# Moving every tile behind a constant by 64 bytes, so that the activations' tiles begin at multiples of 512 bytes

## The chip, the cores and the metric

The kernel runs on one core of one Trainium2 chip. The metric is the device time of one execution in microseconds (us), lower is better. All sizes are float32 unless said otherwise.

## What is computed

A light convolution (a causal filter of 7 taps along the sequence, one filter per head, its weights a softmax over the taps) is followed by a feed-forward layer with a smooth gate. The shapes are x: 8 x 4096 x 192, weight: 8 x 7, w_in: 192 x 2048, w_out: 2048 x 192; so there are 32768 tokens of 192 channels.

```python
def _attn_ref(x, weight):                       # B=8, S=4096, D=192, H=8, K=7
    w = softmax(weight, axis=-1)
    x_pad = np.concatenate([zeros((B, K - 1, D)), x], axis=1)
    idx = np.arange(S)[:, None] + np.arange(K)[None, :]
    x_unf = x_pad[:, idx, :].reshape(B, S, K, H, D // H)
    return np.einsum('hk,bskhg->bshg', w, x_unf).reshape(B, S, D)

def _moe_ref(x, w_in, w_out):
    h = x @ w_in
    g = np.where(h >= 1, h, np.where(h <= -1, 0.0, (h + 1) ** 2 / 4))
    return g @ w_out
```

## The kernel before

**Tiling.** The 32768 tokens are cut into 64 blocks of 512 (`TB`), two blocks making one unit of the convolution; the 2048 features of the hidden layer are cut into 8 pairs of 128 (`NPAIR`). The main loop runs over 512 steps, numbered q = 0 to 511, and two more that drain it: a step is one block and one pair of features. Each step issues three things: the first product `mm1(q)` (L407: hidden features of this pair into a PSUM tile `h`), the second product `mm2` of the step two before (L447: into the PSUM accumulators `accm` and `accr`), and the gate of the present step, which ScalarE and VectorE make out of `h` by way of the SBUF tile `g` (L458 clip, L464 square, L469 max, L476 and L482 split of `g`).

**Precision.** Apart from the first block (and the first eight second products), which use plain float32, a product is made of float32r matmuls with each number split into a high and a low part: activations `hi`/`lo` (and `rhi`, `rlo`, `rh`, `rl` for the last 64 channels) in the first product, `gh`/`gl` in the second, weights in `w` and `wr`. So `mm1` has 18 matmuls in a step and `mm2` 20. Each is 64 rows of the contraction deep (`64*128` in the profile: 64 rows, 128 columns of the array), its stationary operand is 64x128 of `w`, `wr`, and its moving operand is 64x512 of an activation tile. Two matmuls that follow one another use the two halves of the partitions (`HALVES`), and so run side by side on the two halves of the array.

**Beside that.** While the products of one unit run, the convolution of the next one is computed in slots of the same steps: SyncE loads `raw` (L147 turns it into `xT` with VectorE transposes), ScalarE multiplies by a tap (L219), GpSimd adds (L230), the result is split (`hi`, `lo`) and copied to the other half of the partitions by DMAs on SyncE's queue (`hi<-hi`, `lo<-lo`). Accumulators are copied out by ScalarE (L493, L494), added by GpSimd (L496), transposed by VectorE (L519) and stored by SyncE.

**What sets the order.** The order of every engine's work is written out by hand; nothing is planned by costs. Tiles come from pools, which take their places in SBUF one behind the other in the order in which the pools are opened: `const`, `stage`, `xin`, `xw`, `xo`, `act`, `ob`. A tile of the `const` pool is therefore followed by all other pools, and its size moves them. The constant that the change touches is `whose` (L566), which says which channel belongs to which head and is read by four matmuls at the start. It is allocated with 280 columns, of which the first 256 are used:

```python
    wk = const.tile([P, 2, K], F32, name="wk")
    warm = const.tile([P, 1], F32, name="warm")
    whose = const.tile([P, 2 * P + 3 * K + 3], F32, name="whose")[:, 0:2 * P]
    ...
    ident = const.tile([P, P], F32, name="ident")
```

The places that this gives in the program before, in bytes within a partition (each tile's length is a multiple of 32 bytes in its pool):

| tiles | first place | place modulo 512 |
|---|---|---|
| `w0` to `w9`, `wr2` to `wr9`, `wf2` to `wf9` (weights) | 16512 | 128, all of them |
| `whose` | 78048 | 224 |
| `ident` | 79168 | 320 |
| `words`, `m`, `r`, `wa` (weights on their way in) | 79680 | 320 |
| `raw`, three buffers of 2176 bytes | 113472 | 320, 448, 64 |
| `xT`, two buffers of 2176 bytes | 120000 | 192, 320 |
| `y`, `p` (convolution) | 124352 | 448 |
| `hi`, `lo`, `rhi`, `rlo`, `rh`, `rl` (moving operands of the first product) | 134592 | 448, all of them |
| `gh`, `gl`, `g` (moving operands of the second product) | 175552 | 448, all of them |
| `sum`, `osb`, `t` (results on their way out) | 212416 | 448, all of them |

Parts of a weight tile begin at multiples of 512 bytes within it, so every stationary operand of the float32r matmuls begins at 128 modulo 512, and every moving operand at 448 modulo 512, 2048 bytes long.

Of the kernel before, what the change touches and what calls it, by code (L numbers as in the profile page):

```python
# [8 lines left out]
F32 = mybir.dt.float32  # L9
# [9 lines left out]
P = 128  # L19
# [11 lines left out]
def lightconv_then_ffn(ctx: ExitStack, tc: tile.TileContext, x, weight, w_in, w_out, out):  # L31
# [26 lines left out]
    H, K = weight.shape  # L58
# [13 lines left out]
    const = ctx.enter_context(tc.tile_pool(name="const", bufs=1))  # L72
# [491 lines left out]

    wk = const.tile([P, 2, K], F32, name="wk")
    warm = const.tile([P, 1], F32, name="warm")  # L566
    whose = const.tile([P, 2 * P + 3 * K + 3], F32, name="whose")[:, 0:2 * P]
    one = ob.tile([P, TB], F32, name="sum")[:, 0:P]
    small, busy = (ob.tile([P, TB // SQ, SQ], F32, name="osb").rearrange("p j b -> p (j b)")
                    for _ in range(2))  # L570
# [337 lines left out]
```

## Time and profile before

| | |
|---|---|
| three runs, us | 2256.26, 2256.51, 2256.53 (median 2256.51) |
| the profiled execution, first to last instruction, us | 2256.3 |
| PE (matmuls) busy | 2250.8 us, 100% |
| PEld (weight loads, beside the matmuls) busy | 2232.0 us, 99% |
| VectorE busy | 2103.4 us, 93% |
| ScalarE busy | 1697.6 us, 75% |
| GpSimd busy | 1168.5 us, 52% |
| 16 DMA engines busy, main queue | 25.8% |

The page gives the profiled execution its span alone. It is 0.2 us below the median of the runs, so a sum made against the span holds for the time too. A group of the profile reads: line, engine, operation, out<-in by the program's names, shapes, count | busy us in all, mean ns of one | idle time of the engine just before. The profile writes `f32` for float32r where a matmul's operand is meant; which matmuls are float32r follows from the names (`hi`, `lo`, `gh`, `gl` and the like with `w` or `wr`). The busy time of a group of matmuls is the union of its instructions, and matmuls overlap, so counts, not busy times, are added up.

### The profile page before, as it was taken

What the parts mean: (1) busy time and instruction counts of PE and PEld (TensorE: products, weight loads), DVE (VectorE), ACT (ScalarE), POOL (GpSimd) and SP (SyncE); (2) the same over time, 40 slices, a digit from 0 to 9 for tenths busy, and PEclk for the clock granted to TensorE, in tenths of its full rate; (3) what the DMA queues carried; (4) which work ended last, traced back from release to release, by engine and by line L of the source; (5) the groups of instructions that cost most, each with busy time, mean ns of one, the idle gap of its engine ahead of it and who ended that gap; (6) DMA issues with size and microseconds to landing.
All of it is one profiled execution on the core that took longest, in us unless ns stands there. A gap on an engine that the chain in (4) does not pass through costs nothing.

```text
span 2256.3 us, 48204 instructions
## 1 busy us (share of the span) xinstructions
PE 2250.8 (100%) x19646; PEld 2232.0 (99%) x19646; DVE 2103.4 (93%) x1883; ACT 1697.6 (75%) x2153; POOL 1168.5 (52%) x868
## 2 busy tenths in 40 slices
PE   9999999999999999999999999999999999999999
PEld 6999999999999999999999999999999999999999
DVE  8899999999999999999999999999999999999997
ACT  7677877778777787777877777877778777787775
POOL 1546644556445565454654455644556545565441
PEclk9999999999999999999999999999999999999999
DMA  7222222222222212222222222222222222212211
GB/s 158 49 51 46 43 44 49 51 52 39 52 48 46 53 35 51 49 49 51 39 47 47 49 51 49 40 48 45 50 53 39 51 49 46 54 34 51 49 34 24
DMA packets 442125, 110.84 MB, mean 49 GB/s; under 512 B 410288, under 2 KB 417840, under 8 KB 441904
## 3 DMA queue, kind: packets, MB, share of 16 engines
q1 hardware_dynamic: 441744, 107.66, 25.8%
q8 instruction: 155, 2.54, 0.5%
q14 instruction: 66, 0.54, 0.1%
q10 hardware_dynamic: 160, 0.10, 0.0%
HBM read 32.84 MB, written 25.17 MB: 26 GB/s over the span
## 4 chain that ended last, share of the span: by engine, by line
PE 100%; DMA 0%; DVE 0%; ACT 0%; issue 0%; DVEq 0%
PE h L407 47%; PE accm L447 30%; PE accr L447 20%; PE accr L425 1%; PE accm L425 1%; PE accr L190 0%; PE accr L407 0%; PE accm L175 0%; DMA osb<-in_weight_dram 0%; PE h L155 0%; PE accm L181 0%; PE accr L641 0%; PE h L548 0%; PE accm L407 0%; PE accr L548 0%
## 5 line engine op out<-in xcount | busy, mean ns | idle before, releaser
L230 POOL TENSOR_TENSOR y<-y,p 128x512 f32<-128x512 f32 x546 | 765.5, 1402 | 729.4 <-DVE g L469 558.6
L482 DVE TENSOR_TENSOR gl<-g,gh 128x1024 fp32r<-128x1024 f32 (+1 forms) x497 | 732.4, 1474 | 27.5 <-ACT gh L476 23.7
L407 PE MATMUL h<-hi,w 64*128 64x512 f32 x4032 | 740.6, 389 | 0.0
L464 ACT ACTIVATE g<-g 128x1024 f32<-128x1024 f32 (+1 forms) x505 | 535.2, 1060 | 241.8 <-DVE g L458 232.4
L476 ACT CAST gh<-g 128x1024 fp32r<-128x1024 f32 (+1 forms) x497 | 521.7, 1050 | 237.2 <-DVE g L469 223.6
L458 DVE TENSOR_SCALAR g<-h 128x1024 f32<-128x1024 f32 (+1 forms) x505 | 609.7, 1208 | 96.5 <-PE h L407 88.4
L469 DVE TENSOR_TENSOR g<-h,g 128x1024 f32<-128x1024 f32 (+1 forms) x505 | 613.6, 1215 | 11.9 <-ACT g L464 4.5
L447 PE MATMUL accm<-gh,w 64*128 64x512 f32 x3968 | 614.4, 388 | 0.0
L407 PEld LDWEIGHTS h<-hi,w 64*128 64x128 f32 x4032 | 580.3, 184 | 0.0
L407 PE MATMUL h<-lo,w 64*128 64x512 f32 x2016 | 555.9, 388 | 0.0
L447 PEld LDWEIGHTS accm<-gh,w 64*128 64x128 f32 x3968 | 513.1, 184 | 0.0
L447 PE MATMUL accr<-gh,wr 64*128 64x512 f32 x1984 | 387.3, 388 | 0.0
L447 PE MATMUL accm<-gl,w 64*128 64x512 f32 x1984 | 387.3, 388 | 0.0
L447 PE MATMUL accr<-gl,wr 64*128 64x512 f32 x1984 | 387.3, 388 | 0.0
L219 ACT ACTIVATE p<-xT,wk 128x512 f32<-128x512 f32 x562 | 375.0, 709 | 0.0
L407 PEld LDWEIGHTS h<-lo,w 64*128 64x128 f32 x2016 | 350.4, 184 | 0.4 <-DMA lo<-lo 0.2
L407 PE MATMUL h<-rhi,w 64*128 64x512 f32 x992 | 306.0, 388 | 0.0
L407 PE MATMUL h<-rh,w 64*128 64x512 f32 x992 | 306.0, 388 | 0.0
L447 PEld LDWEIGHTS accm<-gl,w 64*128 64x128 f32 x1984 | 286.1, 184 | 0.0
L447 PEld LDWEIGHTS accr<-gh,wr 64*128 64x128 f32 x1984 | 286.0, 184 | 0.0
L447 PEld LDWEIGHTS accr<-gl,wr 64*128 64x128 f32 x1984 | 286.0, 184 | 0.0
L496 POOL TENSOR_TENSOR sum<-t 128x512 f32<-128x512 f32 (+1 forms) x124 | 160.7, 1317 | 127.0 <-ACT t L494 127.0
(143 smaller groups left out, 1975.3 us busy)
## 6 DMA issues: line engine op xcount, KB each, us to landing
out_dram<-osb SPq DMA_DIRECT2D x366, 64.0 KB, 2.0
raw<-in_x_dram SPq DMA_DIRECT2D x334, 68.0 KB, 2.4
hi<-hi SPq DMA_DIRECT2D x126, 128.0 KB, 2.3
lo<-lo SPq DMA_DIRECT2D x126, 128.0 KB, 2.4
rhi<-rh SPq DMA_DIRECT2D x62, 128.0 KB, 2.2
rlo<-rl SPq DMA_DIRECT2D x62, 128.0 KB, 2.3
words<-in_moe_w_in_dram SPq DMA_DIRECT2D x16, 192.0 KB, 3.9
words<-in_moe_w_out_dram SPq DMA_DIRECT2D x8, 384.0 KB, 4.6
```

The costliest lines, as they stand in the source:

```text
L219: nc.scalar.mul(p, self.xT[:, SH + k:SH + k + TB], wk[:, self.wsel, k:k + 1])
L230: nc.gpsimd.tensor_add(y, y, self.product(k))
L407: nc.tensor.matmul(h[e], w[HALVES[e], c0:c0 + P], x[e][e], start=(n == 0), stop=(n == len(mms) - 1))
L425: nc.tensor.matmul(accs[s][a, i][:, c0:c0 + D], g[half, e, b * P:(b + 1) * P], w[half, e, :], start=(j == 0 and e == 0 and b % 2 == 0), st ...
L447: nc.tensor.matmul(accs[s][a, i], st, g[HALVES[i], e, :], start=(j == 0 and n == first[a]), stop=(j == NPAIR - 1 and n == last[a]))
L458: nc.vector.tensor_scalar(out=g[:, e, :], in0=hs[q][:, e, :], scalar1=-1.0, scalar2=1.0, op0=ALU.max, op1=ALU.min)
L464: nc.scalar.activation(g[:, e, :], g[:, e, :], AF.Square, bias=0.5, scale=0.5)
L469: nc.vector.tensor_tensor(out=g[:, e, :], in0=h[:, e, :], in1=g[:, e, :], op=ALU.max)
L476: nc.scalar.copy(gh[:, e, :], gs[q][:, e, :])
L482: eng.tensor_sub(gl[:, e, :], g[:, e, :], gh[:, e, :])
L496: nc.gpsimd.tensor_add(y[:, n], t[0][:, n], t[1][:, n])
```

## The change

`whose` gets 16 more columns, 64 bytes a partition, that nothing reads or writes. Nothing before it moves (the weights stay at 128 modulo 512); `ident` and everything behind it lies 64 bytes further on.

```diff
@@ -564,7 +564,7 @@
     wk = const.tile([P, 2, K], F32, name="wk")
     warm = const.tile([P, 1], F32, name="warm")
-    whose = const.tile([P, 2 * P + 3 * K + 3], F32, name="whose")[:, 0:2 * P]
+    whose = const.tile([P, 2 * P + 3 * K + 19], F32, name="whose")[:, 0:2 * P]
     one = ob.tile([P, TB], F32, name="sum")[:, 0:P]
```

| tiles | modulo 512 before | modulo 512 after |
|---|---|---|
| weights, `whose` | 128, 224 | 128, 224 |
| `ident`, `words`, `m`, `r`, `wa` | 320 | 384 |
| `raw` | 320, 448, 64 | 384, 0, 128 |
| `xT` | 192, 320 | 256, 384 |
| `y`, `p`, `hi` ... `rl`, `gh`, `gl`, `g`, `sum`, `osb`, `t` | 448 | 0 |

No instruction is added, removed or moved on any engine, and no wait changes: the lists of TensorE, VectorE, ScalarE, GpSimd and SyncE are the same in both programs but for the addresses in them.

## The prediction

> **What bounds the kernel now.** I read the page's busy times first, then the chain of work that ended last, then who waited for whom.
>
> ```profile
> span 2256.3 us, 48204 instructions
> PE 2250.8 (100%) x19646; PEld 2232.0 (99%) x19646; DVE 2103.4 (93%) x1883; ACT 1697.6 (75%) x2153; POOL 1168.5 (52%) x868
> PEclk9999999999999999999999999999999999999999
> PE 100%; DMA 0%; DVE 0%; ACT 0%; issue 0%; DVEq 0%
> ```
>
> Of 2256.3 us TensorE has matmuls in the array for 2250.8, at a granted clock of nine tenths or more in every slice, and the chain that ended last is TensorE alone. A busy PE need not be fast, so the next question is whether it ever waits. The waits of PE and PEld, with the largest of the other engines for comparison (engine, tile, line <- releaser: us in all, times, longest):
>
> ```profile
> PE accm L597 <- POOL osb L601: 1.2, 1, 1.2
> PEld h L407 <- issue: 7.1, 32, 0.2
> PEld h L407 <- DMA lo<-lo: 0.2, 1, 0.2
> DVE g L458 <- PE h L407: 88.4, 165, 1.4
> POOL y L230 <- DVE g L469: 558.6, 30, 19.0
> ```
>
> TensorE's longest wait is 1.2 us, once, before the first matmul; its weight loads have one of 0.2 us for a DMA, and 32 pieces of at most 0.2 us, 7.1 us together, that end with nothing the profile shows. It is the others that wait for TensorE (VectorE 88.4 us). So only one thing can move the time by much: the pace at which matmuls follow one another. An engine or a transfer that becomes faster changes nothing, and one that becomes slower matters only once it makes TensorE wait.
>
> The pace, from the timeline of the matmuls (start us, us, ..., count), two steps in the middle:
>
> ```profile
> 999.86 1.24 PE L447 MATMUL accm<-gh,w 64*128 64x512 f32 x8
> ...
> 1004.22 1.24 PE L447 MATMUL accm<-gh,w 64*128 64x512 f32 x8
> ...
> 1008.56 0.78 PE L447 MATMUL accm<-gh,w 64*128 64x512 f32 x4
> ```
>
> Two steps of 38 matmuls take 1008.56 - 999.86 = 8.70 us, 114.5 ns for each; as two run side by side on the two halves of the partitions, a pair of 512 columns takes 228.9 ns. And how many there are, by the groups with their shapes kept apart:
>
> ```profile
> L407 PE MATMUL h<-hi,w 64*128 64x512 f32 x4032 | 740.6, 389 | 0.0
> L407 PE MATMUL h<-lo,w 64*128 64x512 f32 x2016 | 555.9, 388 | 0.0
> L407 PE MATMUL h<-rhi,w 64*128 64x512 f32 x992 | 306.0, 388 | 0.0
> L407 PE MATMUL h<-rh,w 64*128 64x512 f32 x992 | 306.0, 388 | 0.0
> L407 PE MATMUL h<-rl,w 64*128 64x512 f32 x496 | 192.5, 388 | 0.0
> L407 PE MATMUL h<-rlo,w 64*128 64x512 f32 x496 | 192.5, 388 | 0.0
> L447 PE MATMUL accm<-gh,w 64*128 64x512 f32 x3968 | 614.4, 388 | 0.0
> L447 PE MATMUL accr<-gh,wr 64*128 64x512 f32 x1984 | 387.3, 388 | 0.0
> L447 PE MATMUL accm<-gl,w 64*128 64x512 f32 x1984 | 387.3, 388 | 0.0
> L447 PE MATMUL accr<-gl,wr 64*128 64x512 f32 x1984 | 387.3, 388 | 0.0
> ```
>
> The first six make 9024, the last four 9920, together 18944 or 9472 pairs; at 228.9 ns they are 2168 us, 96% of the span. Every one of them reads a moving operand that begins at 448 modulo 512 and a stationary operand at 128, and all ten groups have the same mean of 388 or 389 ns. So the trace of before holds no float32r matmul at another address: their price after the change has to be bounded, not read.
>
> **The change part by part.** Nothing is issued, removed or reordered, so the sum has only address terms.
>
> *Moving operands, 448 to 0 modulo 512 (18944 matmuls).* The nearest rows are the plain float32 matmuls of the first block. Their moving operands lie at two kinds of address: `hi` and `rh` at 448, and `xT` at 436 and 444 (buffer at 320, plus 116 or 124 bytes for taps 3 and 5), which isn't even a multiple of 8. First a window of the groups from 10.99 to 12.1 us, which holds those taps, then the first block's groups and timeline:
>
> ```profile
> L190 PE MATMUL accr<-xT,t 128*128 128x512 f32 x3 | 1.4, 591 | 0.0
> ```
>
> ```profile
> L407 PE MATMUL h<-rh,gh 64*128 64x512 f32 x12 | 3.1, 589 | 0.0
> ```
>
> ```profile
> 16.67 1.88 PE L407 MATMUL h<-hi,gh 64*128 64x512 f32 x8
> 18.39 1.02 PE L407 MATMUL h<-rh,gh 64*128 64x512 f32 x4
> 19.25 1.88 PE L407 MATMUL h<-hi,gh 64*128 64x512 f32 x8
> ```
>
> 591 against 589 ns: no price on the address there. But these matmuls are slower: 12 of them in 19.25 - 16.67 = 2.58 us, 430 ns a pair, so they take a column in about twice the time, and a price that is small against that could be hidden. What float32r would cost at best is half of 430, 215 ns; it takes 228.9. The excess is 13.9 ns a pair, and I can name no wait for it. The bounds for this term follow from it: down to -13.9 ns a pair if the excess is the address's doing and goes, up to +13.9 if the new address brings as much again (the only size of such a stall that the trace has). 9472 x 13.9 ns = 132 us each way. I take 0: the only rows that differ in address, 591 and 589, differ by nothing that could be told apart, and the 13.9 ns has at least one explanation that leaves addresses out. The weight loads run all the time beside the matmuls (PEld 99%), and something of them may cost a matmul that goes at full pace and be hidden behind one at half pace.
>
> *Stationary operands.* They stay at 128 modulo 512: 0 us by themselves. What changes is their distance from the moving operand, which is the second rival's matter.
>
> *VectorE, ScalarE, GpSimd.* They read and write tiles that move by 64 bytes. VectorE's three operations of a step and its transposes:
>
> ```profile
> L482 DVE TENSOR_TENSOR gl<-g,gh 128x1024 fp32r<-128x1024 f32 x495 | 731.1, 1477 | 27.1 <-ACT gh L476 23.2
> L469 DVE TENSOR_TENSOR g<-h,g 128x1024 f32<-128x1024 f32 x503 | 612.3, 1217 | 11.9 <-ACT g L464 4.5
> L458 DVE TENSOR_SCALAR g<-h 128x1024 f32<-128x1024 f32 x503 | 608.4, 1210 | 95.8 <-PE h L407 87.7
> L147 DVE STREAM_TRANSPOSE xT<-raw x95: 464/734/739, 23.8 to 2178.0; 128x544 f32<-128x544 f32 x94, 128x288 f32<-128x288 f32 x1
> ```
>
> The transposes (minimum/median/maximum ns) read `raw` from three buffers at 320, 448 and 64 and write `xT` at 192 and 320; the longest is 739 and the median 734, though the places differ by 128 bytes or more from one to the next. So VectorE shows no price on such a step, and I take 0 for all three engines. The cover if that is wrong: VectorE is idle for 2256.3 - 2103.4 = 152.9 us, so all its work could become 7% slower before TensorE must wait for it throughout; the span would then begin to follow VectorE.
>
> *DMAs.* Their SBUF side now begins at multiples of 128 bytes in `raw` and `osb` and at multiples of 512 in `hi`, `lo`.
>
> ```profile
> DMA packets 442125, 110.84 MB, mean 49 GB/s; under 512 B 410288, under 2 KB 417840, under 8 KB 441904
> q1 hardware_dynamic: 441744, 107.66, 25.8%
> raw<-in_x_dram SPq DMA_DIRECT2D x334, 68.0 KB, 2.4
> lo<-lo SPq DMA_DIRECT2D x126, 128.0 KB, 2.4
> ```
>
> The queue uses 25.8% of the engines, a load or a swap lands 2.4 us after its issue, and TensorE waited 0.2 us for one in the whole run. A gain is hidden behind the matmuls; a loss would have to outlast a step or more before it shows. 0 us, with 0.2 us as the most that can be won.
>
> *Sum.* 0 + 0 + 0 + 0: the span stays at 2256.3 us, and the time at the runs' 2256.5. To tell a change from none the measurement needs about 0.2%, 4.5 us, which here is 4.5 us / 9472 = 0.48 ns a pair. That is a fine scale: any address effect in TensorE that occurs in every matmul would be seen.
>
> **The rivals.** *Faster: the moving operand starts in the middle of what TensorE reads at once.* The excess of 13.9 ns is about a sixteenth of 215 (13.4). If a row of 2048 bytes is read in pieces of 128 bytes, an aligned one has 16, and one that starts at 448 = 3 x 128 + 64 touches 17. Seventeen sixteenths of 215 is 228.4, beside the measured 228.9. After the change every moving operand begins at a multiple of 128 and would have 16. At half pace the extra piece would be hidden, which fits 591 and 589. Against it stands that one coincidence of numbers isn't a mechanism, and that no row shows the pace at another address. Its price: TensorE alone would come down by 132 us to 2124, but VectorE becomes the bound on the way. A step would take 19 x 215 = 4.09 us, while VectorE has 2103.4 / 512 = 4.11 us of work in it, and the two wait for each other through the two buffers of `h`. So I put this case at 2145, between 2124 and 2180.
>
> The Trainium skill bears on this, in "TensorE: Matmul & The Clock Gate", section "Back-to-back issue gap": a warm matmul of N columns follows the last after N/2.4 + 2.5 ns, 215.7 measured at 512 columns. The trace's float32r pairs differ from it by 13.2 ns, and the plain float32 ones agree (430 = 2 x 215). If the change brought the page's pace, the sum would be 9472 x 13.2 ns = 125 us less, 2131 by TensorE alone. The page says nothing of addresses, so it gives the size and not the likelihood.
>
> *Slower: moving and stationary operand meet.* Before, they begin at 448 and 128, 64 apart modulo 128; afterwards at 0 and 128, which is 0 modulo 128. If the memory of a partition lies in interleaved parts that can't be read twice at once, the weight loads that run beside every matmul would now meet the moving operand where so far they missed it. It decides from 0.48 ns a pair on; at one more excess of 13.9 ns the time is 2388. For it speaks that PEld is busy 99% of the span, so there is always a load to meet; against it, that plain float32 pairs overlap with loads just so and hold 430 ns. The Trainium skill speaks against it too: "TensorE: Matmul & The Clock Gate", section "Step-by-step: what each phase is for", gives the moving operand and the weight load two independent read ports. No run here shows whether that holds for two reads of the same part.
>
> **How the numbers follow.** No change: 0.63; its own range is 2252 to 2261. Faster by the pieces of 128 bytes, or by a part of that: 0.24. Slower by meeting operands, or by an engine whose work stretches past VectorE's cover: 0.13. The likeliest is no change, so the predicted time is 2256.5. Its own range holds 0.63, so the range has to reach to one of the others; the faster one adds 0.24, which leaves out 0.13. Low is 2130, near its end by TensorE alone, and high 2262. The chances of faster by over 0.2%, within it and slower by over it are 0.24, 0.63 and 0.13.
>
> **What would show it.** If it stays, the matmuls of a step in the middle still take 4.35 us and all float32r groups keep their 388 ns. If the pieces of 128 bytes are right, the timeline shows a step of about 4.1 us, the mean of a float32r matmul falls by about 13 ns to 375, PE's waits for VectorE (`h` released at L469) appear, and VectorE's wait for `h` at L458 shrinks from 88 us. If the operands meet, 388 grows, in all ten groups alike, and VectorE's wait grows with it. If the transposes at L147, the DMAs' 2.4 us or the additions at L230 move while the matmuls keep their pace, the address has a price that the matmuls hide. What would make the forecast wrong is the one thing the trace can't show, a float32r matmul at another address.

## The result

| | time, us | ratio to before (95% interval) |
|---|---|---|
| before, four runs | 2256.39 (2256.09 to 2256.53) | |
| after, four runs | 2288.86 (2288.50 to 2289.14) | 1.0144 (1.0130 to 1.0159) |

The change makes the kernel 32.5 us slower. The page of the changed kernel, its busy times, clock and chain:

```profile
span 2286.8 us, 48204 instructions
PE 2281.0 (100%) x19646; PEld 2165.4 (95%) x19646; DVE 2094.4 (92%) x1883; ACT 1695.2 (74%) x2153; POOL 1185.1 (52%) x868
PEclk9999999999999999999999999999999999999999
PE 100%; ACT 0%; issue 0%; DVE 0%; DVEq 0%; POOL 0%; POOLq 0%; ACTq 0%
q1 hardware_dynamic: 441744, 107.66, 24.0%
```

TensorE still is the whole chain at the same granted clock, but busy 30.2 us longer with the same 19646 matmuls. VectorE has no more to do than before (2094 against 2103 us), and the DMA queue has less (24.0% against 25.8% of the engines' time), which the kernel gains nothing from. Who waits:

```profile
DVE g L458 <- PE h L407: 119.9, 228, 1.1
PE accm L597 <- POOL osb L601: 1.2, 1, 1.2
PE accr L190 <- ACT xT L168: 0.8, 1, 0.8
PE h L548 <- DVE t L542: 0.2, 1, 0.2
```

The three PE rows are all there are of PE. VectorE waits 31.5 us longer for TensorE than before. So the loss isn't a new wait of TensorE's, it is its pace. The timeline of two steps in the middle, to be held against 999.86, 1004.22 and 1008.56 of before, and the groups:

```profile
1002.62 1.13 PE L447 MATMUL accm<-gh,w 64*128 64x512 f32 x8
...
1007.04 1.13 PE L447 MATMUL accm<-gh,w 64*128 64x512 f32 x8
...
1011.46 1.12 PE L447 MATMUL accm<-gh,w 64*128 64x512 f32 x8
```

```profile
L407 PE MATMUL h<-hi,w 64*128 64x512 f32 x4032 | 667.3, 392 | 0.0
L447 PE MATMUL accm<-gh,w 64*128 64x512 f32 x3968 | 558.5, 392 | 0.0
...
L407 PE MATMUL h<-rh,w 64*128 64x512 f32 x992 | 309.5, 392 | 0.0
...
L407 PE MATMUL h<-rh,gh 64*128 64x512 f32 x12 | 3.1, 589 | 0.0
```

Two steps take 8.84 us where they took 8.70: 232.6 ns a pair instead of 228.9. Taken over the starts of 7000 matmuls in the middle of each trace, which is how the pace of a whole run is worked out below, it is 228.89 before and 232.38 after. All ten float32r groups went from 388 or 389 to 392 ns, the first product as much as the second; the plain float32 matmuls kept their 589. 9472 pairs x 3.49 ns = 33.1 us, against a loss of 32.5. (The spans differ by 30.5 us only, because the profiled execution of before reached its float32 matmuls 2 us later.)

### The profile page after: what moved, and what is told of

Same layout as the page of the kernel before. It is cut to its first block, busy times and chain, and to the rows that moved or that the text cites. A ratio compares the mean times of both kernels' runs of the same rounds, so it can differ in the third digit from the quotient of the medians.

```text
span 2286.8 us, 48204 instructions
## 1 busy us (share of the span) xinstructions
PE 2281.0 (100%) x19646; PEld 2165.4 (95%) x19646; DVE 2094.4 (92%) x1883; ACT 1695.2 (74%) x2153; POOL 1185.1 (52%) x868
## 4 chain that ended last, share of the span: by engine, by line
PE 100%; ACT 0%; issue 0%; DVE 0%; DVEq 0%; POOL 0%; POOLq 0%; ACTq 0%
PE h L407 47%; PE accm L447 30%; PE accr L447 20%; PE accm L425 1%; PE accr L425 1%; PE accr L190 0%; PE accm L597 0%; PE accr L407 0%; PE accm L181 0%; PE h L548 0%; ACT xT L168 0%; ACT xT L165 0%; PE accm L407 0%; PE accr L641 0%; PE h L155 0%
## 5 line engine op out<-in xcount | busy, mean ns | idle before, releaser
L407 PE MATMUL h<-hi,w 64*128 64x512 f32 x4032 | 667.3, 392 | 0.0
L407 PEld LDWEIGHTS h<-hi,w 64*128 64x128 f32 x4032 | 447.0, 185 | 20.6
L447 PEld LDWEIGHTS accm<-gh,w 64*128 64x128 f32 x3968 | 440.5, 185 | 20.5
L407 PE MATMUL h<-lo,w 64*128 64x512 f32 x2016 | 431.8, 392 | 0.0
L447 PE MATMUL accr<-gl,wr 64*128 64x512 f32 x1984 | 327.9, 392 | 0.0
L447 PE MATMUL accr<-gh,wr 64*128 64x512 f32 x1984 | 327.9, 392 | 0.0
L407 PEld LDWEIGHTS h<-lo,w 64*128 64x128 f32 x2016 | 223.8, 185 | 10.4
L447 PEld LDWEIGHTS accr<-gh,wr 64*128 64x128 f32 x1984 | 220.3, 185 | 10.3
L447 PEld LDWEIGHTS accr<-gl,wr 64*128 64x128 f32 x1984 | 220.3, 185 | 10.2
L447 PEld LDWEIGHTS accm<-gl,w 64*128 64x128 f32 x1984 | 220.3, 185 | 10.3
```

Of the source, the lines that this page charges most:

```text
L407: nc.tensor.matmul(h[e], w[HALVES[e], c0:c0 + P], x[e][e], start=(n == 0), stop=(n == len(mms) - 1))
L447: nc.tensor.matmul(accs[s][a, i], st, g[HALVES[i], e, :], start=(j == 0 and n == first[a]), stop=(j == NPAIR - 1 and n == last[a]))
```

## The experiments

Where no interval stands beside a time below, it is that of one execution. Executions of the kernel before, taken beside each group of runs, had medians of 2256.2 to 2256.4 us.

**A false lead: the two halves' distance in time.** The traces differ in a second way. Call partitions 0 to 63 the upper half and 64 to 127 the lower one. A matmul of the lower half starts 163 ns after the one of the upper half that it is paired with before, and 37 ns after it in the changed kernel. The upper half's matmul comes first in each of these two pairs (before, then after):

```profile
1003.53 0.39 PE L407 MATMUL h<-rh,w 64*128 64x512 f32 x1
1003.69 0.39 PE L407 MATMUL h<-rhi,w 64*128 64x512 f32 x1
```

```profile
1001.93 0.39 PE L407 MATMUL h<-rhi,w 64*128 64x512 f32 x1
1001.97 0.39 PE L407 MATMUL h<-rh,w 64*128 64x512 f32 x1
```

The 163 arises at 54.6 us, where TensorE waits 0.2 us for the first swap of `lo`; in the changed kernel that swap lands sooner and the wait is gone. So the address might only have removed a wait, and the pace might go by the distance in time. The rival is the address itself. One edit takes the wait away at the old addresses, one moves all tiles by a whole 512 bytes, and one sets the distance anew 14 times in a run, by an extra matmul whose result is overwritten.

```diff
+            other = nc.scalar if self.c == 0 and name == "lo1" else nc.sync
             nc.sync.dma_start(out=w[TOP].bitcast(F32), in_=t[BOT].bitcast(F32))
-            nc.sync.dma_start(out=w[BOT].bitcast(F32), in_=t[TOP].bitcast(F32))
+            other.dma_start(out=w[BOT].bitcast(F32), in_=t[TOP].bitcast(F32))
```

> The kernel before with all its addresses; only the second DMA of the first swap of lo is issued by ScalarE and not by SyncE, so that it is under way earlier. Phase theory: the one wait of 0.2 us for lo near 54.6 us is gone, the two halves of the array keep starting 36 to 37 ns and not 163 ns apart, a pair of float32r matmuls takes 232.4 ns, and the time is 2288 us (2285 to 2292) although every tile lies where it did. Address theory: tiles stay at 448 modulo 512, so 228.9 ns a pair and 2256 us (2254 to 2258).

Measured: 2257.75 us, ratio 1.0007 (0.9997 to 1.0017), 228.89 ns a pair. The wait for `lo` is gone. The halves came out 88 ns apart and not 37; TensorE has a new wait of 0.9 us before a first product (`PEld h L408 <- PE accr L426`). So this run alone doesn't settle it. The next does.

```diff
-    whose = const.tile([P, 2 * P + 3 * K + 3], F32, name="whose")[:, 0:2 * P]
+    whose = const.tile([P, 2 * P + 3 * K + 131], F32, name="whose")[:, 0:2 * P]
```

> The kernel before with 512 bytes more in the constant, so that every address moves but none modulo 512. Address theory (modulo 512 or less): 2256 us. Phase theory: the time goes by whether the first swap of lo is waited for near 54.6 us: 2256 us with a wait of about 0.2 us and a distance of 163 ns, about 2288 us without it and with 37 ns; which of them cannot be said beforehand.

Measured: 2256.11 us, no wait for `lo`, the halves 21 ns apart with the lower one now first, 228.89 ns a pair. Here they are, in the first product (the lower half's `rhi` and the upper half's `rh`):

```profile
1001.62 0.39 PE L407 MATMUL h<-rhi,w 64*128 64x512 f32 x1
1001.64 0.39 PE L407 MATMUL h<-rh,w 64*128 64x512 f32 x1
1001.85 0.39 PE L407 MATMUL h<-rhi,w 64*128 64x512 f32 x1
```

The wait is gone and the distance is small, and the pace is the old one. The order of the halves is the other way round than in the changed kernel, but a run further on (64 bytes ahead of the weights) has the lower half 30 ns behind, near the changed kernel's 37, and 228.89 ns too. My theory of the distance in time falls.

```diff
+    KICKS = {40 + 32 * i: ((1, 32 * (i + 1)),) for i in range(14)}
 ...
+        for e, cols in KICKS.get(q, ()):
+            w, us, x = mms[0]
+            c0 = COL[us[e]][e]
+            nc.tensor.matmul(h[e][:, 0:cols], w[HALVES[e], c0:c0 + P], x[e][e][:, 0:cols],
+                             start=True, stop=True)
```

> The kernel before with 14 extra matmuls on the lower half of the partitions, one at the head of steps 40, 72, ... 456, of 32, 64, ... 448 columns; their results are overwritten. Each sets the distance between the two halves of the array anew, to about the extra matmul's own length. Phase theory: the pace of a pair changes after an extra matmul and depends on the distance: about 228.9 ns where it is 163 ns and about 232.4 ns where it is 37 ns. Address theory: 228.9 ns a pair in all 15 stretches.

> The changed kernel with the same 14 extra matmuls. Phase theory: the same pace as the kernel before with them at the same distance, so 228.9 ns in some stretches with the activations at 0 modulo 512. Address theory: 232.4 ns in all stretches.

Measured: 2272.24 and 2298.37 us. In the kernel before, the first ten stretches keep 228.89 ns. The extra matmuls add up there: the lower half lies 241 ns behind in the first stretch, then 366, 488 and 586, and 670 to 679, about three matmuls, in the other six. From the extra matmul of 320 columns on it catches up, within 14 steps, until it is ahead by 464 to 495 ns, about two matmuls, and it stays so but for a few steps behind each further extra matmul. These last five stretches run at 232.4 to 233.4 ns, the lowest of them being the one with the turn in it. Two steps of the run, early and late:

```profile
1101.80 0.39 PE L414 MATMUL h<-rhi,w 64*128 64x512 f32 x1
...
1102.47 0.39 PE L414 MATMUL h<-rh,w 64*128 64x512 f32 x1
...
1102.95 0.83 PE L454 MATMUL accm<-gh,w 64*128 64x512 f32 x4
...
1107.29 0.83 PE L454 MATMUL accm<-gh,w 64*128 64x512 f32 x4
```

```profile
2101.41 0.40 PE L414 MATMUL h<-rh,w 64*128 64x512 f32 x1
...
2101.87 0.39 PE L414 MATMUL h<-rhi,w 64*128 64x512 f32 x1
...
2102.34 1.09 PE L454 MATMUL accm<-gh,w 64*128 64x512 f32 x6
...
2106.78 1.09 PE L454 MATMUL accm<-gh,w 64*128 64x512 f32 x6
```

In both steps `rhi` is the upper half's and `rh` the lower half's, which starts 670 ns later in the first step and 460 ns earlier in the second. 4.34 us a step became 4.44. In the changed kernel all stretches lie between 232.4 and 233.4 ns, and none reaches 228.9. So both theories miss. At the old addresses the distance in time doesn't set the pace over a wide range: from 21 ns ahead to 679 ns behind, the lower half goes with 228.9. But the address alone doesn't set it either, since at the old addresses a second, slower rhythm exists, into which a disturbance can push the stream and in which it stays. It was seen only with the lower half about two matmuls ahead. Whether that lead causes the slow rhythm or comes with it is not shown.

**The moving operand's place, or its distance from the stationary one?** Both can explain the result. 64 bytes ahead of the weights move weights and activations alike:

```diff
+    ahead = const.tile([P, 16], F32, name="ahead")
     W = [const.tile([P, 2, n_in[j] + (CW if j >= LAG else 0)], F32R, name=f"w{j}")
```

> The kernel before with 64 unused bytes ahead of the weights, so that weights lie at 192 and activations at 0 modulo 512: the activations' places of the changed kernel, the weights' distance from them as in the kernel before. Theory of the distance (what counts is where the moving operand lies against the stationary one): 228.9 ns a pair, 2256 us. Theory of the place (a moving operand at a multiple of 512 is read more slowly, whatever the weights): 232.4 ns, 2289 us.

Measured: 2255.72 us. The activations lie at multiples of 512 as in the changed kernel, and a step takes 4.34 us as in the kernel before:

```profile
1002.10 1.10 PE L448 MATMUL accm<-gh,w 64*128 64x512 f32 x8
...
1006.44 1.10 PE L448 MATMUL accm<-gh,w 64*128 64x512 f32 x8
```

The alignment isn't what costs; the distance from the weights fits. The counterpart moves the weights alone, by the same line and 448 bytes more in `whose` (`+ 115` for `+ 3`):

> 64 unused bytes ahead of the weights and 448 more in the constant: the weights go from 128 to 192 modulo 512, every activation stays at 448 as in the kernel before. Distance 256, which is 0 modulo 256. Theory of the distance: 226.7 ns a pair and 2235 us, as with 192 bytes more in the constant, though no activation has moved modulo 512. Theory of the activations' place: 228.9 ns and 2256 us.

Measured: 2235.82 us. No activation has moved modulo 512, and the kernel is faster by 20 us:

```profile
1002.60 1.29 PE L448 MATMUL accm<-gh,w 64*128 64x512 f32 x8
...
1006.90 1.29 PE L448 MATMUL accm<-gh,w 64*128 64x512 f32 x8
...
1011.21 1.29 PE L448 MATMUL accm<-gh,w 64*128 64x512 f32 x8
```

**All distances in steps of 32 bytes.** The edit is the one of the 512 bytes with another number (8 for 32 bytes, 24 for 96, and so on, added to the 3).

> 32 bytes more: activations at 480, weights at 128 modulo 512, so the distance is no multiple of 64. If reads go in pieces of 64 bytes or more, neither 228.9 nor 232.4 ns but slower than both, over 2289 us; if in pieces of 32 bytes or less, one of the two: 2256 or 2289 us.

> 128 bytes more in the constant than before: activations at 64, weights at 128 modulo 512. If only the place or distance modulo 128 counts: as before, 228.9 ns and 2256 us. If modulo 512 or more: any pace, 2240 to 2300 us.

> 256 bytes more: activations at 192, weights at 128 modulo 512. If only the place or distance modulo 128 or 256 counts: as before, 228.9 ns and 2256 us. If modulo 512: any pace, 2240 to 2300 us.

> 192 bytes more than before: moving operands at 128, weights at 128 modulo 512, distance 0 modulo 256. Theory of the distance modulo 256 (64 gave 228.9 ns a pair, 96 and 192 gave 233.3, 128 gave 232.4): the two reads begin at the same place of a 256-byte period; if meeting there is what costs, this is as slow as the slowest, 233.3 ns and 2298 us or more. Theory that 64 is the best of all distances: anything from 229 ns on, not under 2254 us.

> 224 bytes more: moving operands at 160, distance 32 modulo 256, the neighbour of 64 on the other side than 96. If the pace has its valley around 64: between 229 and 233.3 ns, 2257 to 2298 us. If only multiples of 64 are good or bad for a reason of their own: 233.3 ns as at 96, 2298 us.

> 96 bytes more: moving operands at 32, distance 160 modulo 256. It lies between 128 (232.4 ns) and 192 (233.3 ns): 232.4 to 233.3 ns and 2289 to 2298 us by the distance theory; if an untried distance frees the matmul of its excess altogether, down to 215.8 ns and about 2140 us.

> 160 bytes more: moving operands at 96, distance 224 modulo 256. Between 192 (233.3 ns) and 0: 233.3 ns and 2298 us by the distance theory; if an untried distance frees the matmul of its excess altogether, down to 215.8 ns and about 2140 us.

> 448 bytes more in the constant: activations at 384, weights at 128 modulo 512, distance 256. Theory of the distance modulo 256: 226.7 ns and 2235 us, as at distance 0. If the period is 512 or longer: another pace, 2250 to 2310 us.

With all runs that change addresses alone, by (moving - stationary) modulo 256:

| distance | moving, stationary modulo 512 | ns a pair | time, us |
|---|---|---|---|
| 0 | 128, 128 (192 bytes more); 384, 128 (448 more); 448, 192 (weights moved) | 226.67 in each | 2235.2; 2234.7; 2235.8 |
| 32 | 160, 128 (224 more) | 233.33 | 2298.3 |
| 64 | 448, 128 (before); 448, 128 (512 more); 0, 192 (both moved); 192, 128 (256 more) | 228.89 in each | 2256.4; 2256.1; 2255.7; 2256.4 |
| 96 | 480, 128 (32 more) | 233.33 | 2298.1 |
| 128 | 0, 128 (after) | 232.38 | 2288.9 |
| 160 | 32, 128 (96 more) | 234.29 | 2307.6 |
| 192 | 64, 128 (128 more) | 233.33 | 2297.9 |
| 224 | 96, 128 (160 more) | 233.33 | 2298.5 |

Seven kernels share two distances, 0 and 64, and each of the two has one pace to 0.01 ns, whatever the operands' own places. The other six distances have one kernel each, so their figure is the rhythm that this run settled in; at 128 the run with extra matmuls showed 232.4 and 233.3 ns. The period is 256: 64 and 320 agree, and 0 and 256. It isn't 128: 0 and 128 differ by 5.7 ns, and so do 64 and 192 by 4.4. Times follow the paces: 9472 x (234.29 - 228.89) = 51 us for the slowest, measured 51.2. Of my expectations, those of 128 bytes more (as before, if the period were 128) and of 192 more (slowest, if meeting at one place costs) missed; the second had the sign wrong. Distance 160 is a little outside the 232.4 to 233.3 expected.

**Does each matmul pay for itself?** 64 bytes between the pools `xo` and `act` move the second product's operands only.

```diff
+    gap = ctx.enter_context(tc.tile_pool(name="gap", bufs=1))
     act = ctx.enter_context(tc.tile_pool(name="act", bufs=2))
 ...
+    between = gap.tile([P, 16], F32, name="between")
```

> 64 bytes between the pools xo and act: the first product's moving operands stay at 448 (distance 64 modulo 256), the second's gh and gl go to 0 modulo 512 (distance 128) as in the changed kernel. If each matmul pays for its own operands: first product 228.9 ns, second 232.4 ns a pair, about 20/38 of the changed kernel's loss: 2256 + 17 = 2273 us. If one sort of matmul drags the other into its rhythm: 2256 or 2289 to 2298 us.

Measured: 2275.63 us, 19.3 more than before, near the 17 expected of half the matmuls. The pace is 230.9 ns over all, 232.1 from matmul to matmul within the second product and 230.2 within the first: the first, whose addresses haven't changed, is a little slower than its 228.9. So neither sort drags the other all the way into its rhythm. That each mostly pays for its own operands, and that the two disturb each other somewhat, fits these figures.

**How firm is the best one?** The extra matmuls again, at distance 0, and a timing:

> The kernel with 192 bytes more (distance 0) and the same 14 extra matmuls on the lower half as in the two runs with extra matmuls before. If the pace of distance 0 doesn't depend on what went before: 226.7 ns a pair in all 15 stretches, 2235 us and 3 to 5 us for the extra matmuls. If an extra matmul can push it into a slower rhythm, as the one of 320 columns did in the kernel before: 226.7 ns at first, and 229 to 233.4 ns from some extra matmul on.

Measured: 2237.32 us, 2 us more than without the extra matmuls, and 226.7 ns in all 15 stretches. At distance 0 none of these disturbances found a slower rhythm. But they only put the lower half further behind, up to 664 ns. It never came ahead, as it did in the slow stretches of the kernel before, so that state is untested here.

> The kernel with 192 bytes more in the constant (distance 0), timed: 2235 us, 0.991 of the kernel before, with an interval that leaves out 1.

Measured: 2235.09 us, ratio 0.9906 (0.9889 to 0.9922). The page and the timeline:

```profile
span 2233.4 us, 48204 instructions
PE 2228.1 (100%) x19646; PEld 2090.2 (94%) x19646; DVE 2093.2 (94%) x1883; ACT 1694.1 (76%) x2153; POOL 1175.6 (53%) x868
```

```profile
1002.10 1.10 PE L447 MATMUL accm<-gh,w 64*128 64x512 f32 x8
...
1006.41 1.10 PE L447 MATMUL accm<-gh,w 64*128 64x512 f32 x8
...
1010.72 1.10 PE L447 MATMUL accm<-gh,w 64*128 64x512 f32 x8
```

4.31 us a step, TensorE is still all of the bound, and VectorE at 94% follows without holding it up. This version beats both kernels.

**Is it the weight load's walk along the memory?** On the changed kernel, the stationary operand is made to stay in one place:

```diff
+                if s > 1:
+                    st = w[HALVES[e], c0:c0 + 1].to_broadcast([P // 2, P])
 ...
+                if s > 1:
+                    st = st[:, 0:1].to_broadcast([P // 2, P])
```

> The changed kernel (distance 128), but from the third block on every weight load reads the first of its 128 columns 128 times, so that it stays in one place of the memory; the products are then of that column alone. If it is the weight load's walk along the memory, beside the moving operand's, that costs: another pace than 232.4 ns, at best 226.7 ns or less (2236 us or less). If only the two start addresses count, or the weight load's place has no part in it: 232.4 ns and 2289 us.

Measured: 2282.74 us, 231.7 ns a pair, 0.7 less than the changed kernel and far from 226.7. The walk isn't what costs most. Whether it has a part stays open: the halves also stand otherwise here, the lower one mostly some 200 ns ahead where it is 37 behind in the changed kernel. What happens between the two reads stays open too.

## Why the prediction was wrong

- **What bounds the kernel: right.** TensorE alone, by its pace. The gains and losses that other engines had are not seen in the time, and the DMAs' gain was hidden, as the sum had it.
- **The step that failed: moving operands, taken at 0.** It measured +3.49 ns a pair, 33.1 us, inside the bounds of 13.9 ns each way that this term had. I took 0 from the float32 rows (591 and 589 ns), which run at half pace. I had written that a price could be hidden there, and took them as evidence all the same. The runs show that float32 rows can't tell. `rh,gh` keeps 589 ns in the changed kernel, though that alone says little: both of its operands move by 64 bytes, and their distance stays 0. With 64 bytes between the pools the distance of this row goes to 192, and it keeps 589 still. The float32 second products (L425, `wf` moving at 128 and `g` stationary) change from distance 192 to 128 with the change. Their rows before, after, and `rh,gh` with the bytes between the pools:

  ```profile
  L425 PE MATMUL accm<-wf,g 64*128 64x192 f32 x256 | 29.3, 322 | 0.0
  ```

  ```profile
  L425 PE MATMUL accm<-wf,g 64*128 64x192 f32 x256 | 27.0, 323 | 0.0
  ```

  ```profile
  L409 PE MATMUL h<-rh,gh 64*128 64x512 f32 x12 | 3.1, 589 | 0.0
  ```

  In the runs of the table L425 met all eight distances, and a pair took 162 or 163 ns (the median) at each.
- **Stationary operands: 0 by themselves, wrong as put.** They don't move, but they set the pace as much as the moving ones do: moving them alone by 64 bytes modulo 512 is worth 20 us.
- **Others at 0: right.** VectorE, ScalarE, GpSimd and the DMAs account for nothing of the loss. The DMA that TensorE waited 0.2 us for came sooner, and the wait went.
- **The rival "slower: moving and stationary operand meet": the kind was right, the size and the place wrong.** It said that the distance counts and that weight loads take part. It had the price four times too high (13.9 ns against 3.5), a period of 128 and not 256, and the worst place at 0, which is the best. I gave it 0.13, and the range ended at 2262, just where it begins (0.48 ns a pair, 4.5 us). The Trainium skill's two independent read ports ("TensorE: Matmul & The Clock Gate", section "Step-by-step: what each phase is for") weighed against it. By this case's runs the pace does depend on how the two reads lie to each other: it goes from 226.67 to 234.29 ns by the distance between them.
- **The rival "faster: pieces of 128 bytes": refuted.** Activations at 0 modulo 512 run at 232.38 with weights at 128 and at 228.89 with weights at 192. That 228.4 lay beside 228.9 was a coincidence. The Trainium skill's 215.7 ns for 512 columns ("TensorE: Matmul & The Clock Gate", section "Step-by-step: what each phase is for"; its formula, in section "Back-to-back issue gap", is given there for an isolated matmul) isn't reached at any distance tried; the best lies 11.0 ns above it.

The range should have reached the slower rival as it did the faster one: the bounds of the unknown term were symmetric, and nothing measured at full pace preferred a side.

## What to carry to other kernels

Where TensorE streams float32r at full pace with a weight load beside every matmul, treat the starts of moving and stationary operands modulo 256 bytes as one parameter, and try all of its values; here, in steps of 32 bytes, distance 0 was best, 64 next, the other six between 232.4 and 234.3 ns, and the spread is 3% of the kernel for some unused bytes in a constant. A tile that only grows or shrinks can so change the time of code that it has nothing to do with. And a price read from matmuls at half pace says nothing of those at full pace: bound it, and give the bound both signs.

## What the runs showed that I had not expected

- The pace of a float32r matmul depends on the distance between its operands modulo 256 bytes, from 226.67 to 234.29 ns a pair; the plain float32 second products of L425 show none of it at any of the eight distances.
- At distance 64 the stream has two rhythms, 228.9 and about 233.3 ns. An extra matmul of 320 columns pushed it into the slower one, and it stayed there for over 800 us and through four more extra matmuls, with the lower half of the array about two matmuls ahead of the upper one. At distance 0 fourteen of them changed nothing. The cause of the rhythms is open.
- The DMA queue's share fell from 25.8 to 24.0% for the same packets and bytes, partly because the span is longer. As time of the 16 engines (share times span) it is 549 us against 582. Over the runs of the table it is 549 or 550 where the activations' tiles lie at multiples of 128 bytes, and 569 to 582 where they lie 64 off such a multiple.
